# Two blocks' loads ahead of two pairs of output weights, and two conversion steps one place earlier, in a fused retention and maxout kernel

## The chip, the cores and the metric

The kernel runs on one core of one Trainium2 chip. Its time is the device time of one execution in microseconds (us), the median over runs. The engines are TensorE (PE, matrix products; its weight loads are listed apart as PEld), VectorE (DVE), ScalarE (ACT), GpSimd (POOL) and SyncE (SP). SP issues every load and store that this text speaks of, in program order, on one queue ("SPq" in the profile).

## The reference

Retention (a causal attention without softmax, with a decay per head) over 8 sequences of 576 positions, 8 heads of 64, and behind it a feed-forward layer that takes the largest of three products. The weights come in double precision (64-bit words), so the kernel has to convert them.

```python
scores = scale * np.matmul(q, k.transpose(0, 1, 3, 2))
gamma = 1.0 - 2.0 ** (-5.0 - np.arange(H, dtype=np.float32))
Dmat = np.where(rel >= 0, gamma[:, None, None] ** rel[None, :, :], 0.0)   # rel = row - column
ret = scores * Dmat[None, :, :, :]
attn_out = np.matmul(ret, v)                                   # (8, 8, 576, 64)
x = attn_out.transpose(0, 2, 1, 3).reshape(4608, 512)
h = np.maximum(np.maximum(x @ w1, x @ w2), x @ w3)             # 512 -> 768
out = h @ w_out                                                # 768 -> 512
```

## The kernel before

The 4608 rows are cut into 36 blocks of 128 rows (the code calls a block `g`) and nine groups of 512 rows, four blocks each (the code calls a group `t`). All instructions stand in an order written out by hand; the engines run their own queues in that order and wait for each other through semaphores. While PE computes the feed-forward layer of group t, the retention of group t + 1 is woven in between its products.

The change lies in the first group, t = 0, the stage from about 27 to 118 us. Three things go on in it at once.

**The feed-forward layer of group 0** (`ffn(0)`). Nine units, each one of the three input weights with one pair of the six 128-column slices of the hidden layer; `up_plain` (L858) makes the products of one slice, and `maximum` (L863) takes the largest into `h` on DVE. Then `downs_plain` multiplies `h` by the output weights `w_out`, slice by slice (L845).

**The weights' conversion** (`convert_all`). It is one long generator; `convert(n)` takes it n steps on. It works on pairs of weight slices (`Two`), 12 of them: nine of the input weights, three of `w_out`, which this text calls p1, p2 and p3. For one pair ACT runs `exponent` (L695, L696) and later `fraction` (L702, L704; DVE's part is L703), DVE runs `whole` (L708), `sign` (L713) and `product` (L728). In the part that matters here two steps always come together: `exponent` of the following pair with `sign` of this one, then `product` of this one; after them `fraction` of the following pair, then its `whole`. `product` ends with `load_weights`, which issues the load of a pair still further on; a pair of `w_out` is two transfers of 512 KB (L516).

**The retention of blocks 4 to 7** (a, b, c and d in the code), for group 1. Each block needs
- `load`: k and v as rows, 256 KB each (L247);
- `load_blocks`: q and k a second time, cut into pieces of 32 positions by 32 channels, 8 transfers of q and 8 of k, 32 KB each (L229; tiles `qraw` and `kxraw`, two buffers each);
- `decay`: v times the decay of its head. For blocks 4 and 5 one DVE instruction does it (L254). For blocks 6 and 7 it is put down as eight ACT instructions, one for each head (L204), in a list that `scale(n)` works off n at a time;
- `transposes`: two DVE instructions that turn the 32 x 32 pieces (L216, `kT` and `qT`);
- `scores`: PE's products of q and k (L322) and of k and v (L325), head by head; `scores` first works off what is left in the list of scalings. DVE masks the scores (L329) and adds up the states (L337), GpSimd scales a state (L339);
- `values`: the products that give the retention's output (L439, L446).

**The order.** `steps(1)` gives 12 places, 0 to 11; the main loop runs what a place lists and then lets `ffn(0)` go on to its next stop. So place n comes ahead of unit n, for n from 0 to 8, and places 9 to 11 lie in `downs_plain`. Inside a unit, `ffn` calls `convert(2)`, `maximum` and `scale(3)` for each of the two slices. In the last unit (the eighth counted from 0) `transposes(d)` stands in the first slice, and the scores of c and d at the end of the second. The order of SP's issues, of ACT's and of DVE's instructions follows from this order of calls.

## Time and profile before

| | |
|---|---|
| median of 3 runs | 739.99 us (739.26 to 740.48) |
| the profiled execution | 739.48 us; its span from first to last instruction 737.8 us |
| granted TensorE clock in it | 1.00 of full speed |
| DVE busy 80 to 85, 85 to 90, 90 to 95 us | 4.08, 4.42, 2.41 us of 5 |
| PE busy 85 to 90, 90 to 95, 95 to 100 us | 5.00, 3.24, 5.00 us of 5 |
| moved 60 to 65, 65 to 70, 70 to 75, 75 to 80, 80 to 85 us | 350, 333, 184, 51, 199 GB/s |
| load of a w_out pair's half (512 KB), issue to landing | 6.0 us (median of six, 3.8 to 8.1) |
| load of 32 KB of a block (L229), issue to landing, in 44 to 102 us | 2.1 us (median, 1.7 to 5.7) |

How to read the profile's lines: a line of the timeline has the start and the duration in us, the engine, the line of the kernel (L858 is line 858), the operation, what it writes and reads, and how many instructions were merged into it (x8). In square brackets is the time that the engine sat idle before it, and what ended the wait. On SPq a duration is how long the issue itself took; the data land later. PE's matmuls in 32-bit floating point appear as two records each.

### The profile page before, as it was taken

How to read it: one execution, taken by the hardware profiler on the slowest of the kernel's cores; microseconds unless marked ns; L12 is line 12 of the kernel's file. 1: busy time of each engine (PE TensorE's matmuls, PEld its weight loads, DVE VectorE, ACT ScalarE, POOL GpSimd, SP SyncE). 2: the span in 40 equal slices, each digit the busy share in tenths (PEclk: the TensorE clock that was granted, in tenths of full speed). 3: DMA queues.
4: the chain of work that ended last, by engine and by line, in shares of the span. 5: the costliest groups of instructions: out<-in, count | busy, mean ns of one | idle time of the engine just before them, and what ended most of it. 6: DMA issues, size and time to landing. Idle time of an engine off the chain costs nothing.

```text
span 737.8 us, 17257 instructions
## 1 busy us (share of the span) xinstructions
PE 731.2 (99%) x6916; PEld 604.5 (82%) x6916; DVE 575.3 (78%) x1050; ACT 352.2 (48%) x734; POOL 37.1 (5%) x43
## 2 busy tenths in 40 slices
PE   9999999999999999999999999999999999999998
PEld 7644546888888888888888888888888888888887
DVE  4899799999886895689658876787768966893676
ACT  4795905554345524544354535543555255424441
POOL 2000010112000100010000000000100010000000
DMA  9878544414251415141424243322514151000001
GB/s 234 270 225 248 113 85 119 83 27 92 70 103 23 95 40 105 36 84 48 102 51 77 47 109 60 65 52 59 114 26 91 44 106 26 1 29 30 1 1 57
DMA packets 234832, 59.90 MB, mean 81 GB/s; under 512 B 220672, under 2 KB 228864, under 8 KB 234752
## 3 DMA queue, kind: packets, MB, share of 16 engines
q1 hardware_dynamic: 233776, 58.76, 35.3%
q8 instruction: 54, 0.88, 0.5%
q14 instruction: 26, 0.21, 0.1%
q10 hardware_dynamic: 976, 0.04, 0.1%
HBM read 49.32 MB, written 9.44 MB: 80 GB/s over the span
## 4 chain that ended last, share of the span: by engine, by line
PE 91%; SPq 5%; DMA 2%; DVE 1%; issue 0%; DVEq 0%
PE a L833 20%; PE b L833 17%; PE c L833 9%; PE di L666 7%; PE d L833 6%; PE e L833 6%; PE dhc L666 5%; PE up L858 3%; PE deg L666 3%; SPq L229 3%; PE sk L322 3%; PE down L845 3%; PE o L439 2%; PE o L446 2%; PE dfd L666 2%; PE dx L573 1%
## 5 line engine op out<-in xcount | busy, mean ns | idle before, releaser
L821 DVE TENSOR_TENSOR part<-part 128x512 f32<-128x512 f32 x168 | 117.8, 701 | 85.9 <-ACT part L818 83.3
L818 ACT COPY part<-b 128x512 f32<-128x512 f32 x120 | 70.3, 586 | 163.2 <-PE b L833 162.7
L821 DVE TENSOR_TENSOR h<-h,part 128x512 f32<-128x512 f32 x120 | 83.2, 694 | 23.8 <-ACT h L818 19.8
L204 ACT ACTIVATE vraw<-vraw,gk 128x64 f32<-128x64 f32 x240 | 77.0, 347 | 11.3 <-DMA vraw<-in_v_dram 11.3
L818 ACT COPY part<-a 128x512 f32<-128x512 f32 x96 | 56.3, 586 | 51.5 <-PE a L833 51.1
L833 PE MATMUL b<-s,n 128*128 128x256 f32 x288 | 73.9, 379 | 0.0
L858 PE MATMUL up<-xT,w 128*128 128x512 f32 (+2 forms) x160 | 62.9, 552 | 0.0
L833 PEld LDWEIGHTS b<-s,n 128*128 128x128 f32 x288 | 54.7, 190 | 7.4
L858 PEld LDWEIGHTS up<-xT,w 128*128 128x128 f32 x160 | 28.8, 190 | 31.5 <-issue 28.6
L339 POOL TENSOR_TENSOR s<-s,gs_of 64x512 f32<-64x512 f32 x24 | 26.4, 1101 | 552.3 <-DVE s L337 512.1
L833 PE MATMUL c<-xT,w 128*128 128x256 f32 x192 | 51.3, 389 | 0.0
L655 ACT COPY k<-di 128x256 f32<-128x256 f32 x49 | 18.3, 373 | 68.5 <-PE di L666 42.1
L833 PE MATMUL d<-s,w 128*128 128x256 f32 x192 | 49.8, 380 | 0.0
L833 PE MATMUL b<-xT,n 128*128 128x256 f32 x192 | 49.3, 379 | 0.0
L833 PE MATMUL a<-xT,w 128*128 128x256 f32 x192 | 49.3, 379 | 0.0
L833 PE MATMUL a<-s,w 128*128 128x256 f32 x192 | 49.3, 379 | 0.0
L833 PE MATMUL a<-xT,n 128*128 128x256 f32 x192 | 45.4, 379 | 0.0
L833 PE MATMUL e<-xT,w 128*128 128x256 f32 x192 | 45.4, 379 | 0.0
L833 PEld LDWEIGHTS e<-xT,w 128*128 128x128 f32 x192 | 36.5, 190 | 5.4 <-issue 0.5
L833 PEld LDWEIGHTS b<-xT,n 128*128 128x128 f32 x192 | 36.5, 190 | 5.0
L833 PEld LDWEIGHTS a<-xT,n 128*128 128x128 f32 x192 | 36.5, 190 | 5.0
L833 PEld LDWEIGHTS a<-xT,w 128*128 128x128 f32 x192 | 36.5, 190 | 5.0
(183 smaller groups left out, 1378.6 us busy)
## 6 DMA issues: line engine op xcount, KB each, us to landing
bits<-in_moe_w_dram SPq DMA_DIRECT2D x9, 1024.0 KB, 7.9
kraw<-in_k_dram SPq DMA_DIRECT2D x32, 256.0 KB, 3.1
vraw<-in_v_dram SPq DMA_DIRECT2D x32, 256.0 KB, 3.9
qraw<-in_q_dram SPq DMA_DIRECT2D x256, 32.0 KB, 2.1
kxraw<-in_k_dram SPq DMA_DIRECT2D x256, 32.0 KB, 2.1
out_dram<-osb SPq DMA_DIRECT2D x56, 128.0 KB, 1.7
bits<-in_moe_w_out_dram SPq DMA_DIRECT2D x6, 512.0 KB, 6.0
out_dram<-osb SPq DMA_DIRECT2D x7, 256.0 KB, 2.0
```

The costliest lines, as they stand in the source:

```text
L204: scaling.popleft()()
L229: nc.sync.dma_start(t[r:r + 32, :, e, :], src[b, :, pos:pos + 32, 32 * a:32 * a + 32].rearrange("h p i -> p h i"))
L322: nc.tensor.matmul(s[half(c), h, :], lhsT=kT[half(c), h, :], rhs=qT[half(c), h, :], start=True, stop=True)
L339: nc.gpsimd.tensor_tensor(new, new, factor, op=ALU.mult)
L439: nc.tensor.matmul(o[m][half(c), n, u, :], lhsT=vds[g][half(m), h, :], rhs=sts[g][half(m), h, :], start=n == 0 and u == 0, stop=place(g, m ...
L655: nc.scalar.copy(place, a)
L666: nc.tensor.matmul(banks[chain], lhsT=hidden(h, order, b, late_ones)[:, e], rhs=late["V"][v][:, e], start=begins and e == 0, stop=chain no ...
L818: nc.scalar.copy(of[step], ps[step[0]][:])
L821: nc.vector.tensor_tensor(of[dst], a, b, op=op)
L833: nc.tensor.matmul(ps[chain][:, e, :], lhsT=factor(w, 2 * fp + e), rhs=xS[t][x], start=n == 1 and e == 0, stop=ends, skip_group_check=True)
L845: nc.tensor.matmul(b[:], lhsT=h[:, fb, m * P:(m + 1) * P], rhs=w_sb["out", fb], start=fb == blocks[0], stop=fb == blocks[-1])
L858: nc.tensor.matmul(ps[:, a:b], lhsT=w_sb[i, fb][:, dc * P:(dc + 1) * P], rhs=xT[t][:, dc, a:b], start=dc == 0 and a == 0, stop=dc == NDC - ...
```

## The change

In the list of places for group 0, block 6's sixteen loads of pieces move from place 6 to place 5, and block 7's from place 7 to place 6. `load_weights` for the second pair of `w_out` is issued by a `product` that is called in between, so block 6's loads now stand ahead of p2 on SP's queue, and block 7's ahead of p3. And `convert(2)` is called once more at place 8, so every conversion step after it is taken two steps sooner than before, and the last call has that much less left.

```diff
             at(4, (transposes, a))
-            at(5, (load, c, "kv"), (decay, b), (transposes, b))
-            at(6, (load, d, "kv"), (decay, c), (load_blocks, c, 0, 1, 2, 3))
-            at(7, (values, [a, b]), (decay, d), (convert, 2), (load_blocks, d, 0, 1, 2, 3))
-            at(8, (transposes, c))
+            at(5, (load, c, "kv"), (load_blocks, c, 0, 1, 2, 3), (decay, b), (transposes, b))
+            at(6, (load, d, "kv"), (load_blocks, d, 0, 1, 2, 3), (decay, c))
+            at(7, (values, [a, b]), (decay, d), (convert, 2))
+            at(8, (transposes, c), (convert, 2))
             at(9, (load, d + 1))
```

What this does to each engine's order, around the change:

```
SP before:  k, v of 6 | p2 | k, v of 7 | pieces of 6 | p3 | pieces of 7 | pieces of 8
SP after:   k, v of 6 | pieces of 6 | p2 | k, v of 7 | pieces of 7 | p3 | pieces of 8

DVE before: transposes of 6, fraction p2, whole p2, maximum, transposes of 7, maximum,
            sign p2, product p2, masks and states of 6 and 7, fraction p3, whole p3, sign p3, product p3
DVE after:  transposes of 6, fraction p2, whole p2, sign p2, product p2, maximum, transposes of 7, maximum,
            fraction p3, whole p3, masks and states of 6 and 7, sign p3, product p3

ACT before: fraction p2, 3 scalings, exponent p3, 1 scaling, fraction p3, 4 scalings (of block 8)
ACT after:  fraction p2, exponent p3, 3 scalings, fraction p3, 5 scalings (one of them of block 7)
```

PE's and GpSimd's orders stay as they are.

## The prediction

> **What bounds the kernel now.** First the page's busy times, then who TensorE (PE) waits for, then the stage of the change engine by engine.

> ```profile
> PE 731.2 (99%) x6916; PEld 604.5 (82%) x6916; DVE 575.3 (78%) x1050; ACT 352.2 (48%) x734; POOL 37.1 (5%) x43
> ```

> PE is idle for 6.6 us of the 737.8 us span, part of it at the start. Whatever makes PE wait longer is added to the end in full, and all that can be won is idle time of PE. The timeline of PE has one such place near the change (start, duration, what, idle before it):

> ```profile
> 94.04 0.33 PE L322 MATMUL sk<-qT,kT 64*64 64x64 f32 x4 [1.76 <-DVE qT L216]
> ...
> 95.35 7.13 PE L845 MATMUL down<-w_out,h 128*128 128x512 f32 x16
> ```

> Scores of block 7 (called d; block 6 is c) start 1.76 us late, because VectorE (DVE) transposes d late, and DVE because d's last load comes late:

> ```profile
> 88.84 0.68 DVE L863 TENSOR_TENSOR h<-h,up 128x512 f32<-128x512 f32 x1
> 92.59 0.71 DVE L216 STREAM_TRANSPOSE kT<-kxraw 128x512 f32<-128x512 f32 x1 [3.07 <-DMA kxraw<-in_k_dram]
> 93.23 0.67 DVE L216 STREAM_TRANSPOSE qT<-qraw 128x512 f32<-128x512 f32 x1
> ```

> So 1.76 us is the most the change can win. What it can lose stands in the two queues whose order it alters. SP's issues (p1, p2, p3 are the three w_out pairs, lines L516; kd, vd the L247 loads of block d):

> ```profile
> 60.89 1.54 SPq L247 DMA_DIRECT2D vraw<-in_v_dram  x1
> 62.97 4.03 SPq L516 DMA_DIRECT2D bits<-in_moe_w_out_dram  x2
> 67.09 0.38 SPq L247 DMA_DIRECT2D kraw<-in_k_dram  x1
> 67.51 1.47 SPq L247 DMA_DIRECT2D vraw<-in_v_dram  x1
> 69.03 6.65 SPq L229 DMA_DIRECT2D qraw<-in_q_dram  x8
> 75.72 5.39 SPq L229 DMA_DIRECT2D kxraw<-in_k_dram  x8
> 81.21 0.87 SPq L516 DMA_DIRECT2D bits<-in_moe_w_out_dram  x2
> 82.13 4.58 SPq L229 DMA_DIRECT2D qraw<-in_q_dram  x8
> 86.75 3.90 SPq L229 DMA_DIRECT2D kxraw<-in_k_dram  x8
> ```

> and ScalarE (ACT), where L695/L696 begin p3's conversion and L204 scales d's v, head by head:

> ```profile
> 86.76 0.81 ACT L204 ACTIVATE vraw<-vraw,gk 128x64 f32<-128x64 f32 x3
> 87.47 1.15 ACT L695 ACTIVATE expo<-bits 128x1024 f32<-128x1024 bf16 x1
> 88.53 1.23 ACT L696 ACTIVATE mant<-bits,one 128x1024 f32<-128x1024 uint32 x1
> 89.65 0.35 ACT L204 ACTIVATE vraw<-vraw,gk 128x64 f32<-128x64 f32 x1
> 89.88 1.15 ACT L702 ACTIVATE expo<-expo,top 128x1024 int32<-128x1024 int32 x1
> 91.07 1.15 ACT L704 ACTIVATE expo<-expo,inf 128x1024 int32<-128x1024 int32 x1
> ```

> The reader is to see that p3 (issued 81.21 and 81.65, landing after 3.8 and 4.72 us, so at 86.37) is read by ACT at 87.47: 1.1 us of slack, and 16 small loads are about to be put ahead of it.

> **The change, part by part.** Nothing is added or removed. Instructions of PE and GpSimd keep their order.

> *DVE.* Sign and product of p2 (1.22 + 1.23 us, L713 and L728, now at 94.39 and 95.63) go ahead of the hidden layer's maximum at 88.84 and d's transposes. In before, DVE idles 3.07 us there for d's load; this idle time covers the 2.4 us. If d is there, DVE goes 88.84 + 2.4 (sign, product) + 0.6 (L863) + 1.2 (two transposes) = 93.1, where before the second transpose ended at 93.9: scores of d could start 0.8 us sooner. In exchange p3's L703 and L708 (0.69 + 1.23 us) come ahead of the masks of c and d. The masks are needed by the values at 102.42, and m of d ended at 99.62; with the numbers below the margin grows, so this costs nothing.

> *ACT.* The three L204 at 86.76 and the one at 89.65 are heads 4 to 6 and 7 of d (16 heads of c and d in all: 3+3+3+3 before them). They now stand behind p3's L695 and L696, and head 7 behind L702 and L704 too. If p3 lands at X (later than 86.8), ACT runs, with the starts above: L695 at X, L696 at X+1.06, heads 4 to 6 from X+2.2, L702 at X+2.9, L704 at X+4.1, head 7 from X+5.15 to X+5.5. Scores of d multiply by scaled v head by head (L325), and the output products (L845) are queued behind them on PE, so these start at about X+5.7 instead of 95.35. That is a loss of **X - 89.65 us**. With p3 landing where it does now there would be no loss. So the sum hangs on X.

> *SP.* c's 16 loads go ahead of p2, d's 16 ahead of p3; both k and v loads keep their places. I price them from rows:
> - What holds the first of a block's 16 loads: c's was held from 69.03 to 72.23 (3.20 us long); the v load ahead of it landed at 67.51 + 6.5 = 74.0, 1.8 us after the release. Block 5's was held from 47.44 to 51.16; its v landed at 44.36 + 8.6 = 52.96, again 1.8 us after. So it is released about 1.8 us before that v lands.
> - From release to the end of 16: block 5 took 51.16 to 58.55, 7.4 us (0.49 us apart); block 6 took 8.9, with one issue of 1.92 us at 76.72 whose reason the trace does not show.
> - A pair lands 4.7 us after its second issue (p3), and k and v behind a pair land 1.8 us after it (p2 at about 72.2, vd at 74.0).
> - Every issue waits for the landing of the one eight places before it (the program uses eight semaphores in turn): d's last q load went at 86.39, right when p3 landed.

> Up to 62.43 the queue is as before. p1 lands at 59.65 + 7.1 = 66.75; without p2 beside it, c's v lands 1.8 later, 68.55. c's loads are released at 66.75 and end at 74.15. p2 is issued at 74.25 and 74.7 and lands at 79.4 (ACT wants it at 81.63: covered by 2.2 us). d's v lands at 81.2, d's loads are released at 79.4 and end at 86.8, landed by 88.6, 3.2 us ahead of DVE. p3 is issued at 86.9 and 87.35 and lands at X = 92.05. With one more late issue like that of 76.72 (1.5 us) X is 93.5. Bounds: if the first loads are not held at all, the eight-place rule still keeps c's last q load until 68.55 and d's until v of d at about 80.0; then 8 issues (3.9 us), the pair (0.45) and 4.72 give X = 89.55. If c's v lands as in before (69.8) and both blocks have a late issue, X = 92.05 + 1.25 + 3.0 = 96.3. Between these I take the rows of held loads, which held both times that weights stood ahead, and half a late issue: X = 92.8.

> The later loads (block 8) are issued from about 88 instead of 90.75, so nothing behind p3 gets later. p3's product, L728, would come by about 103 on DVE and is used by PE after 114.

> **Sum.** 92.8 - 89.65 = 3.15 us of longer PE stall, nothing given back, since PE has no idle time behind it. The profiled execution took 739.48 us (span 737.8 and 1.7 around it), so 742.6; the median of the runs, 739.99, lies 0.5 above that execution, and I forecast 742.9 between the two footings.

> **Rivals.**
> - *The loads flow better* (same within what can be told). The first loads are held little, X between 88.9 and 91.1, loss -0.8 to +1.5 us; the middle is 739.9. For it: only L229 issues of this size behind weights were seen held, and the held one of block 8's q row (90.75, 4.80 us for eight) lost just 0.9. Against: the two rows with weights, k and v ahead.
> - *The gain comes* (not slower). If p3 lands by 88.85, heads are scaled by 94.4 and the 0.8 us of DVE's earlier transposes is kept: 739.48 - 0.8 = 738.7; at most 1.76 us, 737.7. It decides at X = 89.65, where loss becomes gain. For it: 16 loads at the bare 0.49 us are 7.9 us per block. Against: the eight-place bound of 89.55.
> - *PE comes back slowly.* At the kernel's start four transposes of k (L286) took 1.09 us at 4.02 and 0.66 us at 8.44: from 1.12 to 5.85 PE ran at about 0.6 of its later pace, 1.9 us lost, though the granted clock reads 1.00 there. In the forecast PE idles 1.0, 1.6 and 2.5 us with 0.9 us of work between. If that sets the slow pace in again: 742.6 + 1.9 = 744.5, and up to 746 with a late issue. Against: after the 1.76 us of idle the next products are at their pace. [...]
> - *The order does not act*: if SP did not issue in the listed order, nothing would change, 739.5. The listing of the program's order shows the moves on SP, ACT and DVE, so this is small.

> **How the numbers follow.** Forecast (X 91.1 to 96.3, +1.5 to +6.6 us) 56%; loads flow better 20%; gain 10%; slow pace 11%; order does not act 3%. About 0.2% (1.5 us) is what a measurement tells from no change. Faster by more than that needs nearly all of the 1.76 us: 5%. Within it: flow better, most of the gain case and no action, with some rest of the forecast's low end: 25%. Slower: 70%. The range 739.9 to 746.0 leaves out the gain and the low half of the first rival (some 14%) and a slow pace on top of two late issues (5%). The forecast's own range is 741.0 to 746.0.

> **What would show it.** Right: on SP the last w_out pair issued at about 87 instead of 81; ACT's L695 idle some 6 us before it, put down to bits of w_out; two stalls of PE inside scores of block 7, released by ACT L204; L845 starting near 98.5; d's transposes not waiting for a load. Wrong: p3 landing before 89.6, or scores of d that end before 95.35; a first q load that is not held; L845 matmuls of more than the 0.45 us a piece of now (7.13 us for 16), which would be the slow pace.

## The result, and the profile after

| | before | after |
|---|---|---|
| median of 9 runs | 739.99 us (737.46 to 743.53) | 745.11 us (743.01 to 746.90) |
| the profiled execution's span | 737.8 us | 743.4 us |
| its mean granted clock | 1.000 | 0.995 |
| scores of block 7 over, L845 starts (from unit 7's first product) | 18.16 us | 21.95 us |
| L845's first 16 records | 7.13 us | 9.08 us |
| unit 7's first product to the next group's first (L833) | 41.09 us | 46.81 us |

The change makes the kernel slower: ratio 1.0068 (interval 1.0048 to 1.0089). The last line of the table holds all of it: 5.72 us, and the spans differ by 5.6. It has two parts, 3.79 us up to the start of L845 and 1.95 us in L845's first 16 records.

SP's timeline of the changed kernel (start, duration of the issue, what):

```profile
60.76 1.33 SPq L247 DMA_DIRECT2D vraw<-in_v_dram  x1
62.54 8.01 SPq L229 DMA_DIRECT2D qraw<-in_q_dram  x8
70.59 3.90 SPq L229 DMA_DIRECT2D kxraw<-in_k_dram  x8
74.59 0.87 SPq L516 DMA_DIRECT2D bits<-in_moe_w_out_dram  x2
75.56 0.38 SPq L247 DMA_DIRECT2D kraw<-in_k_dram  x1
75.98 0.58 SPq L247 DMA_DIRECT2D vraw<-in_v_dram  x1
76.61 7.22 SPq L229 DMA_DIRECT2D qraw<-in_q_dram  x8
83.87 3.90 SPq L229 DMA_DIRECT2D kxraw<-in_k_dram  x8
87.87 0.87 SPq L516 DMA_DIRECT2D bits<-in_moe_w_out_dram  x2
```

Each block's 16 loads hold SP for 11 to 12 us (before, 12.1 and 8.5), and the last pair of w_out leaves at 87.87 and 88.3 instead of 81.21 and 81.65. Its second half takes 4.8 us to land, so the pair is there at 93.1.

ACT and DVE of the changed kernel (in brackets the idle time before, and what ended it):

```profile
86.83 1.15 ACT L704 ACTIVATE expo<-expo,inf 128x1024 int32<-128x1024 int32 x1
93.17 1.18 ACT L695 ACTIVATE expo<-bits 128x1024 f32<-128x1024 bf16 x1 [5.20 <-DVE qT L216]
94.24 1.22 ACT L696 ACTIVATE mant<-bits,one 128x1024 f32<-128x1024 uint32 x1
95.33 0.83 ACT L204 ACTIVATE vraw<-vraw,gk 128x64 f32<-128x64 f32 x3
96.04 1.15 ACT L702 ACTIVATE expo<-expo,top 128x1024 int32<-128x1024 int32 x1
97.23 1.15 ACT L704 ACTIVATE expo<-expo,inf 128x1024 int32<-128x1024 int32 x1
98.28 0.33 ACT L204 ACTIVATE vraw<-vraw,gk 128x64 f32<-128x64 f32 x1
```

```profile
91.77 0.70 DVE L216 STREAM_TRANSPOSE kT<-kxraw 128x512 f32<-128x512 f32 x1
92.40 0.67 DVE L216 STREAM_TRANSPOSE qT<-qraw 128x512 f32<-128x512 f32 x1
```

DVE's transposes of block 7 no longer wait for a load. ACT now idles 5.2 us ahead of L695. The bracket names DVE's transpose, which happened to end at 93.07; L695 reads nothing of it, but reads the pair that landed at 93.1, and where the transpose ends earlier (below) the same wait is put down to the load. Behind L695 stand the scalings of heads 4 to 6 and, after two more conversion steps, of head 7. PE shows what that costs:

```profile
93.21 0.33 PE L322 MATMUL sk<-qT,kT 64*64 64x64 f32 x4 [0.99 <-DVE qT L216]
95.74 0.27 PE L325 MATMUL kv<-vraw,kraw 64*64 64x64 f32 x2 [1.60 <-ACT vraw L204]
98.67 0.48 PE L325 MATMUL kv<-vraw,kraw 64*64 64x64 f32 x4 [1.96 <-ACT vraw L204]
99.08 9.08 PE L845 MATMUL down<-w_out,h 128*128 128x512 f32 x16
```

There are three waits, of 0.99, 1.60 and 1.96 us, in place of one of 1.76; that is 2.79 us more. The scores of block 7 themselves run for 2.31 us instead of 1.31, split by the waits into stretches of 0.93, 0.97 and 0.41 us; from about 96.2 they run at a granted clock of 0.50. Then L845 takes 0.57 us a record instead of 0.45. The windows of one microsecond show the clock (busy times of PE, PEld, DVE, ACT, POOL, then the granted clock, the DMA share and GB/s):

```profile
95.00:96.00 1.00, 0.26 (x12) 0.23 (x12) 0.52 (x1) 1.00 (x4) 0.00 (x0) 1.00 0.33 52
96.00:97.00 1.00, 0.70 (x24) 0.49 (x16) 1.00 (x2) 1.00 (x2) 0.00 (x0) 0.60 0.43 67
...
102.00:103.00 1.00, 1.00 (x3) 0.47 (x2) 0.96 (x2) 0.93 (x4) 1.00 (x1) 0.50 0.48 74
103.00:104.00 1.00, 1.00 (x3) 0.38 (x2) 1.00 (x1) 0.14 (x1) 0.54 (x1) 0.99 0.43 67
```

From about 96.2 to 103 the granted clock is one half; in the profiled execution of before it is 1.00 throughout.

### The profile page after: what moved, and what is told of

Its sections match the earlier page's. It is cut to its first block, busy times and chain, and to the rows that moved or that the text cites. A ratio compares the mean times of both kernels' runs of the same rounds, so it can differ in the third digit from the quotient of the medians.

```text
span 743.4 us, 17259 instructions
## 1 busy us (share of the span) xinstructions
PE 733.2 (99%) x6916; PEld 604.9 (81%) x6916; DVE 575.1 (77%) x1050; ACT 352.3 (47%) x734; POOL 40.6 (5%) x43
## 4 chain that ended last, share of the span: by engine, by line
PE 94%; SPq 3%; DMA 2%; ACT 1%; issue 0%; DVE 0%; ACTq 0%
PE a L833 20%; PE b L833 17%; PE c L833 9%; PE up L858 7%; PE di L666 7%; PE d L833 6%; PE e L833 6%; PE dhc L666 5%; PE deg L666 3%; PE sk L322 3%; PE down L845 3%; PE o L439 2%; PE o L446 2%; PE dfd L666 2%; PE dx L573 1%; SPq L229 1%
## 5 line engine op out<-in xcount | busy, mean ns | idle before, releaser
L204 ACT ACTIVATE vraw<-vraw,gk 128x64 f32<-128x64 f32 x240 | 77.0, 347 | 4.5 <-DMA vraw<-in_v_dram 4.5
L833 PE MATMUL b<-s,n 128*128 128x256 f32 x288 | 73.9, 379 | 0.0
L833 PEld LDWEIGHTS b<-s,n 128*128 128x128 f32 x288 | 54.7, 190 | 7.4
L833 PE MATMUL c<-xT,w 128*128 128x256 f32 x192 | 51.3, 389 | 0.0
L833 PE MATMUL d<-s,w 128*128 128x256 f32 x192 | 49.8, 380 | 0.0
L833 PE MATMUL a<-s,w 128*128 128x256 f32 x192 | 49.3, 379 | 0.0
L833 PE MATMUL a<-xT,w 128*128 128x256 f32 x192 | 49.3, 379 | 0.0
L833 PE MATMUL b<-xT,n 128*128 128x256 f32 x192 | 49.3, 379 | 0.0
L833 PE MATMUL e<-xT,w 128*128 128x256 f32 x192 | 45.4, 379 | 0.0
L833 PE MATMUL a<-xT,n 128*128 128x256 f32 x192 | 45.4, 379 | 0.0
L833 PEld LDWEIGHTS e<-xT,w 128*128 128x128 f32 x192 | 36.5, 190 | 5.4 <-issue 0.5
L833 PEld LDWEIGHTS a<-s,w 128*128 128x128 f32 x192 | 36.5, 190 | 5.0
L833 PEld LDWEIGHTS a<-xT,n 128*128 128x128 f32 x192 | 36.5, 190 | 5.0
L833 PEld LDWEIGHTS a<-xT,w 128*128 128x128 f32 x192 | 36.5, 190 | 5.0
```

Of the source, the lines that this page charges most:

```text
L204: scaling.popleft()()
L833: nc.tensor.matmul(ps[chain][:, e, :], lhsT=factor(w, 2 * fp + e), rhs=xS[t][x], start=n == 1 and e == 0, stop=ends, skip_group_check=True)
```

## The experiments

The theory is that the late pair holds ACT, and PE waits for the scalings behind it; PE's idle time then halves the clock. Rivals: the loads cost by their new place alone, the conversion steps cost by theirs, or the clock falls for another reason. "Stage" is the time from unit 7's first product to the next group's first, of the profiled execution: 41.09 us before, 46.81 after. The start of the kernel differs by up to 1.6 us from execution to execution, so the stage tells more than the span. The experiments ran in three sets on three chips, each set beside runs of the kernel before: 740.23 us (35 runs), 741.06 (23 runs) and 740.96 (18 runs).

**Only the loads.** The conversion stays where it was.

```diff
-            at(5, (load, c, "kv"), (decay, b), (transposes, b))
-            at(6, (load, d, "kv"), (decay, c), (load_blocks, c, 0, 1, 2, 3))
-            at(7, (values, [a, b]), (decay, d), (convert, 2), (load_blocks, d, 0, 1, 2, 3))
+            at(5, (load, c, "kv"), (load_blocks, c, 0, 1, 2, 3), (decay, b), (transposes, b))
+            at(6, (load, d, "kv"), (load_blocks, d, 0, 1, 2, 3), (decay, c))
+            at(7, (values, [a, b]), (decay, d), (convert, 2))
```

> Only the loads move; the conversion keeps its old places. Theory (p3's late landing holds ACT, and d's scalings wait behind ACT's read of p3): p3 lands near 93 as in the changed kernel, but only d's last head (one L204) stands behind L695 and L696, and L702 and L704 come after it. d's transposes end by about 91, so PE starts d's scores at once and waits only in its last head, until 93.1 + 2.2 + 0.5 = 95.8; L845 starts near 95.9 instead of 95.35: +0.5 us, about 740.5, clock full (one idle time of about 2.4 us). Rival (the loads' new place costs by itself): about +5 us as the changed kernel.

Measured: 743.63 us against 740.23, ratio 1.005 (1.003 to 1.007); stage 43.24 us. ACT and PE of this kernel:

```profile
93.55 1.15 ACT L695 ACTIVATE expo<-bits 128x1024 f32<-128x1024 bf16 x1 [4.38 <-DMA bits<-in_moe_w_out_dram]
94.61 1.19 ACT L696 ACTIVATE mant<-bits,one 128x1024 f32<-128x1024 uint32 x1
95.71 0.33 ACT L204 ACTIVATE vraw<-vraw,gk 128x64 f32<-128x64 f32 x1
```

```profile
96.09 0.33 PE L325 MATMUL kv<-vraw,kraw 64*64 64x64 f32 x4 [2.16 <-ACT vraw L204]
96.36 8.82 PE L845 MATMUL down<-w_out,h 128*128 128x512 f32 x16
```

Here the wait is put down to the load of w_out. L845 starts 0.47 us later than before, counted from unit 7 (18.63 against 18.16 us): the stall is what the theory said. But L845's first 16 records took 8.82 us, because the clock fell here too, after a single wait of 2.16 us:

```profile
96.00:97.00 1.00, 0.91 (x5) 0.69 (x6) 0.93 (x3) 1.00 (x2) 0.00 (x0) 0.69 0.42 65
...
99.00:100.00 1.00, 1.00 (x3) 0.47 (x2) 0.97 (x2) 0.00 (x0) 0.31 (x1) 0.61 0.43 67
```

So in this execution 1.69 us of the 2.15 us lost are the clock. It was one of the fastest (742.18 us); what the slower ones lost beyond that (up to 748.17 us), no trace shows. The step of the expectation that a wait of that length would leave the clock full is refuted.

**Only the conversion steps.**

```diff
-            at(8, (transposes, c))
+            at(8, (transposes, c), (convert, 2))
```

> Only the two conversion steps move; all loads as before. Theory: p3 lands at 86.4, before ACT reaches L695 at 86.8, so no head of d is late; d's transposes wait for d's load until 92.6 as before; PE as before: 0 us, within 0.3 us, about 740. Rival (the conversion ahead of the transposes costs by itself): +2.4 us of DVE work on the path, about 742.4.

Measured: 741.01 against 740.23, ratio 1.0004 (0.9988 to 1.0021); stage 40.45 us, 0.6 shorter than before. The pair had landed when ACT came to it, so L695 at 88.27 has no wait in front; PE's wait ahead of block 7's scores was 1.11 us:

```profile
88.27 1.15 ACT L695 ACTIVATE expo<-bits 128x1024 f32<-128x1024 bf16 x1
```

```profile
94.88 0.33 PE L322 MATMUL sk<-qT,kT 64*64 64x64 f32 x4 [1.11 <-DVE qT L216]
```

The steps cost nothing by themselves that these runs can tell. The loads alone cost 3.4 us of the change's 5.1 us; the rest needs both, the late pair and the steps that put more scalings behind it.

**The changed kernel with the scalings first.** In the last unit `scale` is called ahead of `convert`, so that d's last four heads are scaled before ACT reads the late pair.

```diff
-                        convert(4 if (fp, i) == units[1] else 2)
+                        scale(8 if (fp, i) == units[8] else 0); convert(4 if (fp, i) == units[1] else 2)
```

> The changed kernel, but with d's last four scalings ahead of p3's conversion on ACT in the last unit. p3 stays late (near 93) and holds ACT, but nobody on PE waits for it. Theory: L845 starts near 94.5, PE's only stall is some 1.0 us for d's transposes, full clock: -0.8 us against before, about 739.2. Rival (the stall has another cause than the scalings behind p3, or the late p3 is needed elsewhere): most of the +5 us stays.

Measured: 739.67 against 740.23, ratio 0.9989 (0.9973 to 1.0004): the whole loss is gone, and a gain is not told apart from none; stage 40.50 us, 0.6 shorter than before. ACT:

```profile
88.57 1.05 ACT L204 ACTIVATE vraw<-vraw,gk 128x64 f32<-128x64 f32 x4
93.95 1.13 ACT L695 ACTIVATE expo<-bits 128x1024 f32<-128x1024 bf16 x1 [4.34 <-DMA bits<-in_moe_w_out_dram]
```

The pair is as late as in the changed kernel and ACT waits for it as long, but nobody waits for ACT. PE keeps one wait of 1.01 us. This shows the mechanism of the stall: not the late pair itself, but what is queued behind its first reader. It also rules out that the burst of transfers by itself lowers the clock: from 90 to 93 us this kernel moved 303, 406 and 287 GB/s, the changed one 369, 373 and 259, and only one of its 12 runs had a lowered clock.

**Only block 6's loads.** Block 7's stay behind p3, and the conversion where it was.

```diff
-            at(5, (load, c, "kv"), (decay, b), (transposes, b))
-            at(6, (load, d, "kv"), (decay, c), (load_blocks, c, 0, 1, 2, 3))
+            at(5, (load, c, "kv"), (load_blocks, c, 0, 1, 2, 3), (decay, b), (transposes, b))
+            at(6, (load, d, "kv"), (decay, c))
```

> Only block 6's loads go ahead of p2; block 7's stay behind p3, conversion at its old places. Theory: p2 is issued near 74.6, p3 right behind d's k and v near 77 and lands near 84.6, before ACT needs it; d's loads run from about 78 to 89, held by the eight-place rule until p3 lands, and have landed near 91: d's transposes some 1.5 us sooner than before and no new wait: -1.5 us, about 738.5. Rival (any load ahead of the w_out pairs costs): slower than before by 1 us or more.

Measured: 739.58 against 740.23, ratio 1.0003 (0.9982 to 1.0024); stage 41.04 us, as before. The gain of 1.5 us that was expected did not come. SP of this kernel:

```profile
78.21 4.51 SPq L516 DMA_DIRECT2D bits<-in_moe_w_out_dram  x2
82.77 4.99 SPq L229 DMA_DIRECT2D qraw<-in_q_dram  x8
87.80 3.90 SPq L229 DMA_DIRECT2D kxraw<-in_k_dram  x8
```

Issued right behind p2 and d's k and v, the two halves of p3 took 4.51 us to issue instead of 0.87, so d's loads began only at 82.77, as late as before, and PE waited 1.71 us.

**All loads moved, the conversion where it was, the scalings first.** The diffs of the first and the third experiment together, on the kernel before.

> All loads moved as in the change, the conversion at its old places, and d's last scalings ahead of the conversion on ACT in the last unit. Theory: d's transposes find their data (end near 91.5 us), all heads are scaled by 90, and p3's late landing (near 93) holds only ACT's conversion, which PE needs after 110. No stall of PE is left between the scores of c and d: -1.76 us against before. And if idle time of PE is what takes the granted clock to half for 3.4 us at a time, it stays at 1.00 in nearly all runs, where before has 0.995 to 0.998 in about a third: mean near 738.3 against 740.3. Rival (the late pair costs elsewhere): no gain, or slower.

Measured: 739.41 against 741.06, ratio 0.9979 (0.9966 to 0.9992): a little faster than the kernel before, and so than the changed one, which was not run beside it. Stage 40.00 us, 1.1 shorter than before. DVE and PE:

```profile
92.57 0.71 DVE L216 STREAM_TRANSPOSE kT<-kxraw 128x512 f32<-128x512 f32 x1 [1.97 <-DMA kxraw<-in_k_dram]
```

```profile
94.02 0.33 PE L322 MATMUL sk<-qT,kT 64*64 64x64 f32 x4 [0.66 <-DVE qT L216]
95.33 7.13 PE L845 MATMUL down<-w_out,h 128*128 128x512 f32 x16
```

The expected 1.76 us came to 1.1, since d's loads landed later in this execution than in the changed kernel's (they left by 11.9 us after unit 7's start, there by 10.6) and DVE waited for them after all. Of the 1.5 us between the means (739.5 against 741.0), 0.65 is left between the runs of both kernels with a clock of 0.999 or 1.000 (739.35 against 740.0); the rest is that fewer runs lost clock, 1 of 12 against 12 of 23.

**The changed kernel with idle work in PE's waits.** This adds products of the identity, into a tile that nobody reads: 7 ahead of head 4's kv product of block 7, and 9 ahead of head 7's.

```diff
+            if g == 2 * CPT - 1 and h in (4, 7):
+                fill = ps_y.tile([P, P], FP32, tag="y", name="fill")
+                for _ in range(7 if h == 4 else 9):
+                    nc.tensor.matmul(fill[:], lhsT=ident[:], rhs=ident[:], start=True, stop=True)
             for c in kept:
```

> The changed kernel with idle work on PE in the two waits for ACT: 7 products of the 128x128 identity ahead of head 4's kv product of block 7 and 9 ahead of head 7's (about 0.21 us each, 1.5 and 1.9 us), into a PSUM tile that nobody reads. The waits stay as long, so L845 starts as late as in the changed kernel (3.7 us later than before, up to 0.5 more). Theory (PE's idle time took the clock to half for 6.6 us, which cost 1.95 us in L845): granted clock 1.000, L845's first 16 records back at 7.1 us, total +3.7 to +4.2, about 744, against +5.7. Rival (the clock falls for another reason, such as the time of the DMA burst): clock 0.995 as in the changed kernel, +5.7.

Measured: 746.69 us over 6 runs, against 741.06, ratio 1.0073 (1.0051 to 1.0095); stage 46.96 us.

```profile
94.27 0.33 PE L322 MATMUL sk<-qT,kT 64*64 64x64 f32 x4 [1.62 <-DVE qT L216]
95.29 3.18 PE L327 MATMUL fill<-ident 128*128 128x128 f32 x14
99.12 2.27 PE L327 MATMUL fill<-ident 128*128 128x128 f32 x18
101.59 7.13 PE L849 MATMUL down<-w_out,h 128*128 128x512 f32 x16
```

The experiment was badly sized. The first wait, ahead of the scores, was not filled and took 1.62 us here; the clock fell at about 95.5, the first filler ran at half pace (3.18 us for 14 records) and pushed the rest back. The clock was full again by L845 (7.13 us) although the stall was the longest so far, and none of the 6 runs had 0.995, which 7 of the changed kernel's 9 had. Five of the 6 still had 0.997 or 0.998. On the total it decides nothing.

**The same with all three waits filled**, by 4, 6 and 8 products.

```diff
+        fills = {0: 4, 4: 6, 7: 8} if g == 2 * CPT - 1 else {}
+        if 0 in fills:
+            fill(fills[0])
...
+            if h > 0 and h in fills:
+                fill(fills[h])
```

> The changed kernel with idle products in all three waits of PE inside the scores of block 7, each a little shorter than the wait (4, 6 and 8 identity products of 0.21 us: 0.85 us ahead of the first score, 1.3 ahead of head 4's kv product, 1.7 ahead of head 7's), so that the waits end no later. Theory (the half clock comes from PE's idle time): granted clock 1.000 in most runs, L845's first 16 records 7.1 us, from unit 7's products to the next layer's first 3.7 us longer than before instead of 5.7 (up to 5 where p3 lands a microsecond later): mean near +4 against before's undisturbed runs. Rival (something else in that time lowers the clock): 0.995 to 0.998 in most runs.

Measured: 745.83 over 7 runs against 740.96, ratio 1.0053 (1.0033 to 1.0073). Three of the 7 runs had a clock of 0.999 or 1.000 and took 744.0 on average; four had 0.997 or 0.998 and took 746.3. None of the changed kernel's 9 runs had more than 0.998. In the profiled execution the pair landed at 96.1, 2.0 us later against unit 7 than in the changed kernel's, so a wait of 1.72 us stayed, and the clock fell after it:

```profile
98.76 0.27 PE L335 MATMUL kv<-vraw,kraw 64*64 64x64 f32 x2 [1.72 <-ACT vraw L204]
99.51 3.12 PE L318 MATMUL fill<-ident 128*128 128x128 f32 x16
```

The three runs at full clock lie 4.0 us above before's at full clock (740.0), close to the stall of 3.8 us in the changed kernel's trace; their own stalls were not traced, and in the profiled execution L845 started 6.65 us later than before. The result is in part as expected.

**The kernel before with idle work.** 7 products between the scores of c and of d, where PE idles 1.76 us.

```diff
+            if g == 2 * CPT - 1 and h == 0:
+                fill = ps_y.tile([P, P], FP32, tag="y", name="fill")
+                for _ in range(7):
+                    nc.tensor.matmul(fill[:], lhsT=ident[:], rhs=ident[:], start=True, stop=True)
```

> The kernel before with 7 products of the identity (1.5 us) on PE between the scores of c and d, where it idles 1.76 us. Theory (idle time of PE lowers the clock, in a third of the runs of before): the stage takes as long as in an undisturbed run of before, but runs with a clock under 0.9985 become rare: mean near 739.4 against 740.3, smaller spread. Rival (the clock's falls come from elsewhere, the start for instance): as many runs under 0.9985 as before, mean unchanged or up to 0.5 us longer.

Measured: 740.17 (739.61 to 740.97, 12 runs) against 741.06 (738.79 to 743.12), ratio 0.9991 (0.9979 to 1.0003). The medians are not told apart, but the clock is: all 12 runs had 0.999 or 1.000, where 12 of before's 23 runs beside them had 0.998 or less. The mean, 740.2, is close to that of before's runs at full clock on the same chip (740.0).

```profile
92.69 1.83 PE L324 MATMUL fill<-ident 128*128 128x128 f32 x14
95.81 7.13 PE L849 MATMUL down<-w_out,h 128*128 128x512 f32 x16
```

So by these runs it is in this wait that the clock is lost, in the kernel before too, and with work in it the clock was kept.

**The best version so far with 3 such products** ahead of d's scores.

```diff
+        fills = {0: 3} if g == 2 * CPT - 1 else {}
+        if 0 in fills:
+            fill(fills[0])
```

> The loads of the change, conversion at its old places, d's scalings first, and 3 identity products (0.64 us) ahead of the scores of block 7, where the version without them idled 0.66 us. Theory: stage 1.1 to 1.7 us shorter than before, clock at 1.000 in all runs: mean 1.3 to 2 us under before's, a little under the version without the products. Rival (the products delay d's scores where its data come in time): 0.6 us longer than without them, mean gain under 1 us.

Measured: 739.58 against 740.96, ratio 0.998 (0.9968 to 0.9993), not told apart from the version without them. In its profiled execution d's transposes ended before PE needed them, so the products only took their 0.6 us: stage 39.91 us. And 3 of 12 runs still had 0.998, against 1 of 12 without the products; where these runs lost it, no trace shows.

## Why the prediction was right, point by point

- **The direction and the place** held: the loss lies in one queue on SP that pushes p3 back, ACT that reads p3 ahead of d's scalings, and PE that waits for them.
- **SP's sum** held within a microsecond. Block 6's loads ended at 74.49 (predicted 74.15), p2 left at 74.59 (74.25), block 7's ended at 87.77 (86.8), p3 landed at X = 93.1 (92.05, and 92.8 with half a late issue). The first loads were released at 66.36 and 79.55 (66.75 and 79.4). The late issue of 1.92 us did not come back; in its place each block had a shorter one, of 1.17 us at 67.39 and 1.28 us at 79.59, where the others took 0.45. The one in block 7 is most of what X was later than 92.05, so the half late issue in the sum stood for something real, but that its size was right is luck. The terms listed for the lower bound add up to 89.07; its 89.55 comes out only with the last q load's own issue of 0.48 us, which is not listed.
- **The loss as X - 89.65** held: X = 93.1 gives 3.45, measured 3.79. The scalings ran where the working put them (head 7 at X + 5.2). The rest is for the most part head 7's products, which already ran at a clock of 0.50: 0.41 us from 98.67 to the start of L845, where the working had 0.2.
- **DVE's 0.8 us** held: d's transposes ended at 93.07 (93.1), and the profiled execution with the scalings first kept 0.6 us of gain.
- **The step that was mis-sized** is the last term of the sum, the pace of PE after the stall. It was taken as unchanged in the forecast, and the slow pace was a rival with 11% and a price of 1.9 us. It cost 1.95 us in the trace, and all 9 runs had a lowered clock. 3.15 + 1.95 = 5.1 us would have met the 5.1 us between the medians. That the price fits is luck: the 1.9 us came from 4.7 us of slow products at the kernel's start, the 1.95 us from the part of 6.8 us of half clock that fell on L845. The rival spoke of three gaps, of 1.0, 1.6 and 2.5 us; with only the loads moved, half a clock followed a single wait of 2.16 us. The argument against it, that the clock was full after the 1.76 us of idle time in before, rested on one execution; 36 of the 76 runs of before that stand beside the experiments had 0.998 or less.
- **The gain as a rival** (p3 landing early enough) did not come. Once the scalings stand first, the stage of the profiled executions is 0.6 to 1.1 us shorter; in the runs at full clock it shows only with the conversion at its old place (739.35 against 740.0, and 739.4 against 740.0 with three products added), and not with the conversion moved as well (739.6 against 739.4). Gain and lower half of the first rival make 20% by the prediction's own chances, where it says that some 14% lie below its range.

## What to carry to other kernels

Before a load is moved ahead of another on one queue, ask who reads the one that becomes late, and what stands behind that reader on its engine; here four small scalings behind one conversion step made a 6.7 us delay of off-path weights into a stall of PE, and putting them first took the loss away. Small loads had a price in queue time wherever they stood (16 of 32 KB held SP for 7.7 to 12.1 us in the trace of before), so moving them moves the lateness. And count idle time of PE twice: once for itself, and once for the clock behind it (in the changed kernel's trace 2.79 us more of waits, and 1.95 us more in L845's first 16 records).

## What the runs showed of the hardware

The table has PE's waits in the one profiled execution of each kernel, and how many of all its runs had a mean granted clock of 0.998 or less; how long the waits were in the other runs is not known.

| kernel | waits of PE among the scores | runs at 0.998 or less |
|---|---|---|
| before, filled | none | 0 of 12 |
| loads, scalings first, filled | none | 3 of 12 |
| loads, scalings first | 0.66 us | 1 of 12 |
| changed, scalings first | 1.01 | 1 of 12 |
| conversion only | 1.11 | 6 of 12 |
| block 6 only | 1.71 | 4 of 12 |
| before | 1.76 | 36 of 76 (13 of 35, 12 of 23, 11 of 18 by chip) |
| changed, two waits filled | 1.62 | 5 of 6 |
| changed, three waits filled | 0.25 + 1.72 | 4 of 7 |
| loads only | 2.16 | 11 of 12 |
| changed | 0.99 + 1.60 + 1.96 | 9 of 9 |
